# Attention beside a token-mixing MLP on one core: scores and product sums share four PSUM banks in turn, and the MLP's products are dealt evenly over the pairs of steps

## The chip, the core and the metric

One NeuronCore of a Trainium2 chip runs the whole program. The metric is the device time of one execution in microseconds; lower is better. Engines are named as the profile names them: PE (TensorE, matrix products; PEld are its weight loads), DVE (VectorE), ACT (ScalarE), POOL (GpSimd), SP (SyncE, which issues most DMAs). PE writes its results to PSUM, which has eight banks, each of 128 partitions by 512 float32 values; DVE or ACT reads a result from there, and only then may PE write to that bank again.

## What is computed

```python
x = A_x                                   # 2048 tokens x 512 channels
xn = _layernorm(x, axis=-1)
qkv = xn @ wqkv                           # 32 heads of 16
p = _softmax(q @ k.T * 16 ** -0.5)        # for each head, 2048 x 2048
s = (p @ v) @ wo
h = _layernorm(xn, axis=-1)
u = _gelu(h.T @ w1 + b1)                  # MLP across tokens, 2048 -> 1792
y = u @ w2 + b2                           # 1792 -> 2048
g = _silu(y.T)
out = x + s * g
```

Everything is float32. The big products are made three times, with an upper and a lower part of each factor (hi*hi, hi*lo, lo*hi), so one product of two blocks is three matmuls.

## The kernel before

**Stages.** First come the layer norms and the projections to q, k and v. Then a loop over steps in pairs, `for s in range(0, total + 1, 2)`. At step s the *maxima* of step s are made, and the *scores* of step t = s - 22, and the *values* of t - 2. From s = 22 to s = 510 every pair of steps has all of them; these are the 245 pairs that the change is about. Before them (s < 22) there are only maxima, behind them (s >= 512) only scores and values.

**One pair of steps** on PE is made of:

- eight maxima (`max_of`, L494): 48 x 128 by 48 x 512, into a bank of the pool `ps_mx`, which DVE reduces to a row maximum (L498). `ps_mx` has three banks.
- eight scores (`score`, L872): 50 x 128 by 50 x 512, into a bank of `ps_sc`, which ACT turns into exponentials (L877). `ps_sc` has three banks.
- two groups of values (`values`, L888), each of four matmuls in four column tiles (each of them two records in the trace), into the one bank of `ps_av`.
- zero to six products of the MLP or of the last projection (L1039), which are added up in the one bank of `ps_dn`. Each is made in two halves of 64 rows.

Maxima, scores and halves of products use 64 rows of the array or fewer. They are issued in *slots* of two, one for each half of the array's rows, and the two run at the same time. Which kinds stand in a pair's slots is written out by hand, as two strings for the two halves (D a product's half, m a maximum, s a score) and the two slots ahead of which a group of values stands. These rows are in `ORDERS`, and for pairs in which a sum ends or behind such a pair in `ENDS` and `BEGINS`. A pair with n products has 8 + n slots.

**Products.** `mixer()` yields the products of 14 sums of the first layer (48 products each) and of 16 sums of the second (42 each); `rest()` yields 13 sums of the last projection (9 each) and what comes after the loop. Ahead of the 245 pairs 177 products are done, and 1284 remain. A sum's end yields a function that reads the bank: `gelu` (first layer, ACT at L579, then POOL), `silu` (second layer) or `part` (last projection). Behind it `mixer` yields `None`, which ends the pair's share: the next sum starts in the next pair, since there is one bank for sums. `count` says how many products a pair takes: six, or four in pairs behind a sum's end and where seven or eight are left (in the fifth to the eighth sum always six).

**The second layer's input.** The results of the first layer go to DRAM (`store`, `u_d`) and come back to the tiles that held the first layer's input. The last of them comes back inside the first sum of the second layer, ahead of its last block: `mixer` waits there until it is stored, issues the load (L555), and yields `None` twice.

**Other work of DVE.** Every eighth pair ends a block of maxima. `max_rows` then reduces them (L513) and turns them by four 32 x 32 transposes (L510), in three pieces at the next three places ahead of values.

## Time and profile before

| | |
|---|---|
| median of 3 runs | 1676.91 us (1676.75 to 1678.35) |
| span of the profiled execution, first to last instruction | 1673.9 us |
| time of that execution outside the span | not in the record; the median is 3.0 us above the span |
| PE busy | 1658.1 us (99%) |
| DVE busy | 1428.2 us (85%) |
| ACT busy | 1200.1 us (72%) |
| POOL busy | 560.1 us (33%) |
| the 245 pairs | 206.35 to 1591.60 us, 1385.25 us |

Busy time of PE is the union of its instructions' spans. Matmuls are pipelined, and the spans that are shown overlap, so 99% busy does not mean that PE works at its peak: a matmul that starts late while an earlier one is still shown leaves no idle time in this number. The starts of the matmuls say more. In the views of windows, each row has the window, its length, and for each engine the busy time and the number of instructions.

### The profile page before, as it was taken

What the parts mean: (1) busy time and instruction counts of PE and PEld (TensorE: products, weight loads), DVE (VectorE), ACT (ScalarE), POOL (GpSimd) and SP (SyncE); (2) the same over time, 40 slices, a digit from 0 to 9 for tenths busy, and PEclk for the clock granted to TensorE, in tenths of its full rate; (3) what the DMA queues carried; (4) which work ended last, traced back from release to release, by engine and by line L of the source; (5) the groups of instructions that cost most, each with busy time, mean ns of one, the idle gap of its engine ahead of it and who ended that gap; (6) DMA issues with size and microseconds to landing.
All of it is one profiled execution on the core that took longest, in us unless ns stands there. A gap on an engine that the chain in (4) does not pass through costs nothing.

```text
span 1673.9 us, 30821 instructions
## 1 busy us (share of the span) xinstructions
PE 1658.1 (99%) x11754; PEld 874.6 (52%) x11754; DVE 1428.2 (85%) x2497; ACT 1200.1 (72%) x2300; POOL 560.1 (33%) x663
## 2 busy tenths in 40 slices
PE   9999999999999999999999999999999999999997
PEld 8887645454454445544444544445454444444443
DVE  7665988888888989889998989899898998899945
ACT  3333277777777777777877777777777778888875
POOL 0223853342234332342322322222223222642421
PEclk9999999999999999999999999999999999999999
DMA  6478621505142241916141513123142515363345
GB/s 231 178 239 188 130 65 46 92 28 85 39 72 60 50 68 34 242 55 105 36 83 39 95 49 53 48 54 66 36 67 62 84 37 93 117 124 103 115 143 201
DMA packets 152176, 155.30 MB, mean 93 GB/s; under 512 B 51596, under 2 KB 109964, under 8 KB 148956
## 3 DMA queue, kind: packets, MB, share of 16 engines
q1 hardware_dynamic: 147612, 152.59, 37.7%
q8 instruction: 92, 1.51, 0.4%
q0 software_dynamic: 4416, 0.75, 0.3%
q14 instruction: 56, 0.46, 0.1%
HBM read 101.86 MB, written 50.32 MB: 91 GB/s over the span
## 4 chain that ended last, share of the span: by engine, by line
PE 97%; DVE 2%; ACT 1%; issue 0%; DMA 0%; DVEq 0%; SPq 0%
PE av L888 30%; PE dn L1039 23%; PE mx L494 17%; PE sc L872 13%; PE dn L998 3%; PE mx L397 2%; PE sc L397 2%; DVE mxp L498 1%; PE av L998 1%; PE av L397 1%; PE dn L397 1%; PE mx L872 1%; PE sc L86 0%; PE sc L88 0%; PE sc L87 0%; PE mx L88 0%
## 5 line engine op out<-in xcount | busy, mean ns | idle before, releaser
L498 DVE TENSOR_REDUCE mxp<-mx 128x1 f32<-128x512 f32 x2004 | 1243.5, 682 | 146.7 <-PE mx L494 106.3
L877 ACT ACTIVATE prob<-sc 128x512 f32<-128x512 f32 x2004 | 1050.3, 604 | 300.5 <-PE sc L872 195.7
L872 PE MATMUL sc<-big 50*128 50x512 f32 x2004 | 755.5, 418 | 0.6
L494 PE MATMUL mx<-big 48*128 48x512 f32 x2004 | 744.5, 421 | 0.7
L888 PE MATMUL av<-prob,vp 128*32 128x512 f32 x4096 | 545.7, 605 | 0.0
L1039 PE MATMUL dn<-hu,wh 64*128 64x512 f32 x1556 | 538.9, 406 | 0.0
L494 PEld LDWEIGHTS mx<-big 48*128 48x128 f32 x2004 | 358.6, 185 | 284.0 <-DVE mxp L498 262.5
L872 PEld LDWEIGHTS sc<-big 50*128 50x128 f32 x2004 | 358.5, 185 | 102.0 <-ACT prob L877 82.5
L1039 PE MATMUL dn<-hu,wl 64*128 64x512 f32 x778 | 316.7, 407 | 0.0
L1039 PEld LDWEIGHTS dn<-hu,wh 64*128 64x128 f32 x1556 | 284.4, 184 | 44.4 <-issue 23.8
L1039 PEld LDWEIGHTS dn<-hu,wl 64*128 64x128 f32 x778 | 143.5, 185 | 108.0 <-issue 79.7
L888 PEld LDWEIGHTS av<-prob,vp 128*32 128x32 f32 x4096 | 80.8, 108 | 177.2 <-issue 166.1
L79 POOL TENSOR_TENSOR wl<-raw,wh 128x512 fp32r<-128x512 f32 x124 | 150.8, 1219 | 38.7 <-ACT wh L150 30.2
L148 POOL CAST wh<-raw 128x512 fp32r<-128x512 f32 (+1 forms) x107 | 62.1, 580 | 269.8 <-PE dn L1039 185.2
L521 POOL CAST m<-f 16x128 fp32r<-16x128 f32 x32 | 9.0, 280 | 278.6 <-DVE f L510 278.6
L580 POOL TENSOR_TENSOR sq<-u 128x512 f32<-128x512 f32 x14 | 14.6, 1041 | 178.4 <-ACT u L579 178.4
L83 POOL DMA_DIRECT2D big<-m x128 | 67.7, 535 | 0.0
L1039 PE MATMUL dn<-wh,hu 64*128 64x512 f32 x156 | 55.4, 408 | 0.0
L616 POOL TENSOR_SCALAR t<-t 128x512 f32<-128x512 f32 x16 | 23.8, 1490 | 79.8 <-ACT t L613 79.8
L79 POOL TENSOR_TENSOR hu<-hx,hu 128x512 fp32r<-128x512 f32 x16 | 20.4, 1292 | 67.1 <-ACT hu L255 67.1
L877 ACT ACTIVATE prob<-mx 128x512 f32<-128x512 f32 x44 | 27.4, 623 | 13.4 <-PE sc L872 11.5
L397 PE MATMUL mx<-xt,big 128*128 128x512 f32 x144 | 34.6, 389 | 0.0
(228 smaller groups left out, 1122.5 us busy)
## 6 DMA issues: line engine op xcount, KB each, us to landing
raw<-in_B_w_dram SPq DMA_DIRECT2D x104, 256.0 KB
big<-k_d SPq DMA_DIRECT2D x96, 128.0 KB
big<-q_d SPq DMA_DIRECT2D x96, 128.0 KB
q_d<-sg SPq DMA_DIRECT2D x16, 512.0 KB
k_d<-sg SPq DMA_DIRECT2D x16, 512.0 KB
num_d<-ev SPq DMA_DIRECT2D x30, 256.0 KB
u_d<-uo SPq DMA_DIRECT2D x14, 512.0 KB
hu<-u_d SPq DMA_DIRECT2D x14, 512.0 KB
```

Of the source, the lines that this page charges most:

```text
L79: eng.tensor_tensor(out=o, in0=a, in1=b.bitcast(F32), op=OP.subtract)
L83: queue.dma_start(dst.bitcast(F32), src.bitcast(F32))
L148: nc.gpsimd.tensor_copy(whs[n][:, :m, :], raws[n][:, :m, :])
L397: nc.tensor.matmul(ps, w[part][:, kd, m], xt[kd][:, z, :], start=w is wh and z == 0 and kd == 0, stop=w is wl and kd == ND - 1,)
L494: nc.tensor.matmul(ps, q[o : o + 48, r * P : (r + 1) * P], k[o : o + 48, c * 512 : (c + 1) * 512], start=True, stop=True,)
L498: nc.vector.tensor_reduce(mxp[u // 16][:, a, r % 8, c : c + 1], ps, axis=AX.X, op=OP.max)
L616: nc.gpsimd.tensor_scalar(t, t, 1.0, None, op0=OP.add)
L872: nc.tensor.matmul(ps, ks[p][o : o + 50, kb * P : (kb + 1) * P], qs[p][o : o + 50, at : at + 512], start=True, stop=True,)
L877: nc.scalar.activation(e, ps, AF.Exp, scale=scale)
L888: nc.tensor.matmul(av[32 * j : 32 * j + 32, :], vps[p][:, kb, 16 * a : 16 * a + 32], prob.pop((t, a, c)), start=kb == 0, stop=kb == NB - 1,)
L998: nc.tensor.matmul(ps, w(slice(0, P)), m(slice(0, P)), start=first, stop=last)
L1039: made.append(lambda r=r, start=first and a == lead, stop=last and a != lead: nc.tensor.matmul(ps, w(r), m(r), start=start, stop=stop,))
```

## The change

1. **Four banks in turn.** `ps_sc` (three banks) and `ps_dn` (one) become a ring of four pools of one bank each. `turn()` hands out the next bank of the ring and leaves out banks on which a sum is under way. A sum takes its bank (`Sum`) when its first product is issued, and keeps it until its last one is issued (`let_go`).
2. **No break at a sum's end.** The `None` behind a sum is gone in the 245 pairs, so that the next sum can start in the same or the next pair.
3. **Even shares.** `plan` works out ahead of the pairs by which pair each sum is to end, evenly, and the 13 sums of the last projection by two pairs each; `count` takes what is left of the sum by the pairs that are left to it, at most six.
4. **New orders.** `MIDST`, `BEGIN` (behind a pair in which a sum ended) and `END` (such a pair) take the place of `ORDERS`, `BEGINS` and `ENDS`.
5. **The last load of the second layer's input** is issued at the first block of products at which it is stored, and no `None` follows it.

The number of pairs with n products, before: 149 with six, 14 with five, 79 with four, and one each with three, one and none. After: 72 with six, 160 with five, 13 with four. The sum is 1284 both times.

```diff
-    ps_sc = pool("ps_sc", 3, space=PSUM)
+    ring = [pool(f"ps_{i}", 1, space=PSUM) for i in range(4)]
     ps_mx = pool("ps_mx", 3, space=PSUM)
     ps_av = pool("ps_av", 1, space=PSUM)
-    ps_dn = pool("ps_dn", 1, space=PSUM)
...
+    def turn(lasting=False):
+        while True:
+            place[0] = (place[0] + 1) % 4
+            if place[0] not in summing:
+                break
+        if lasting:
+            summing.append(place[0])
+        return ring[place[0]].tile([P, 512], F32, name="sc")
+
+    class Sum:
+        def __init__(self, of=lambda: turn(True)):
+            self.of, self.ps = of, None
+        def __call__(self):
+            if self.ps is None:
+                self.ps = self.of()[:, :D]
+            return self.ps
...
-                if i == NF and kb == NF - 1:
-                    while NF - 1 not in stored:
+                if i == NF and len(ub) < NF:
+                    while kb == NF - 1 and NF - 1 not in stored:
                         yield None
-                    ub.append(hu.tile([P, 2, D], F32R, name="hu"))
-                    move(ub[NF - 1], u_d[NF - 1])
-                    yield None
-                    yield None
+                    if NF - 1 in stored:
+                        ub.append(hu.tile([P, 2, D], F32R, name="hu"))
+                        move(ub[NF - 1], u_d[NF - 1])
...
-            yield (lambda i=i, ps=ps: gelu(i, ps)) if i < NF else (lambda i=i, ps=ps: silu(i - NF, ps))
-            if i + 1 >= min(N_BEFORE, NF):
-                yield None
+            yield let_go((lambda i=i, ps=ps: gelu(i, ps())) if i < NF else (lambda i=i, ps=ps: silu(i - NF, ps())), not (before and i % 2))
+
+    def let_go(f, lasting=True):
+        def then():
+            if lasting:
+                summing.pop(0)
+            f()
+        return then
...
-        6: ("DDDDDDsmmsmsms", "msmssmmsDDDDDD", 4, 8),
+        5: ("DDDDDmmssmsms", "msmsmssmDDDDD", 5, 8),
...
+    END = {5: ("DDDDDssmmsmsm", "smsmsmmsDDDDD", 5, 8), 6: ("DDDDDDsmssmmsm", "smsmmsmsDDDDDD", 7, 14)}
...
+    def plan():
+        left = -done
+        of = []
+        for n in sizes:
+            left += n
+            if left > 0:
+                of.append(left)
+                left = 0
+        pairs = (NU - LEAD) // 2 - 2 * PARTS
+        n = pairs / sum(of[:-PARTS])
+        at = 0
+        for i, size in enumerate(of):
+            at += size
+            short = i - len(of) + PARTS + 1
+            last_pairs.append((done + at, pairs + 2 * short if short > 0 else round(at * n)))
...
-        if i in FULL:
-            return max(0, min(6, left))
-        return 4 if late or left in (7, 8) else 5 if left == 9 else max(0, min(6, left))
+        end, pair = last_pairs[0]
+        return min(6, (end - done) // max(1, pair - k))
```

The order on PE shows it at two places and the one on SP at a third. Names are as the program gives them: `mx` a bank for a maximum, `sc` one for a score (and, after the change, for a sum too), `dn` a sum's bank before, `av` the values' bank, `big` the tiles of q and k, `hu` the MLP's input, `wh` and `wl` the upper and lower part of its weights.

**First place: PE, a common pair in the second layer's sums, from behind the first group of values to the first matmul of the second.** Before (a pair with six products):

```order
L1039 MATMUL dn_14345<-hu_9176,wl_14349 128x512
L872 MATMUL sc_14704<-big_1495,big_1496 128x512
L1039 MATMUL dn_14345<-hu_9255,wh_14348 128x512
L494 MATMUL mx_14709<-big_1386,big_1385 128x512
L872 MATMUL sc_14712<-big_1495,big_1496 128x512
L494 MATMUL mx_14716<-big_1386,big_1385 128x512
L494 MATMUL mx_14719<-big_1386,big_1385 128x512
L872 MATMUL sc_14722<-big_1495,big_1496 128x512
L888 MATMUL av_14214<-prob_14624,vp_12874 32x512
```

After, in the same pair, which now has five:

```order
L524 MATMUL mx_14693<-big_1392,big_1391 128x512
L908 MATMUL sc_14696<-big_1501,big_1502 128x512
L524 MATMUL mx_14700<-big_1392,big_1391 128x512
L908 MATMUL sc_14703<-big_1501,big_1502 128x512
L908 MATMUL sc_14707<-big_1501,big_1502 128x512
L524 MATMUL mx_14711<-big_1392,big_1391 128x512
L924 MATMUL av_14200<-prob_14655,vp_12862 32x512
```

Between the two groups of values four slots became three: no product stands there any more, and three maxima follow each other in successive slots.

**Second place: PE, the end of the fifth sum of the first layer and the start of the next.** Before:

```order
L494 MATMUL mx_3058<-big_1496,big_1495 128x512
L1039 MATMUL dn_2412<-hu_153,wh_2497 128x512
L494 MATMUL mx_3062<-big_1496,big_1495 128x512
L1039 MATMUL dn_2412<-hu_153,wh_2497 128x512
L494 MATMUL mx_3066<-big_1496,big_1495 128x512
L1039 MATMUL dn_2412<-hu_153,wl_2498 128x512
L888 MATMUL av_2939<-prob_2947,vp_1667 32x512
L888 MATMUL av_2939<-prob_2965,vp_1667 32x512
L888 MATMUL av_2939<-prob_2986,vp_1667 32x512
L888 MATMUL av_2939<-prob_2995,vp_1667 32x512
L1039 MATMUL dn_3080<-hu_138,wh_2669 128x512
L494 MATMUL mx_3088<-big_1496,big_1495 128x512
```

After:

```order
L524 MATMUL mx_3133<-big_1502,big_1501 128x512
L1076 MATMUL sc_2424<-hu_159,wh_2578 128x512
L908 MATMUL sc_3137<-big_1391,big_1392 128x512
L1076 MATMUL sc_2424<-hu_159,wh_2578 128x512
L524 MATMUL mx_3142<-big_1502,big_1501 128x512
L1076 MATMUL sc_2424<-hu_159,wl_2579 128x512
L924 MATMUL av_2942<-prob_3056,vp_1673 32x512
L924 MATMUL av_2942<-prob_3065,vp_1673 32x512
L924 MATMUL av_2942<-prob_3017,vp_1673 32x512
L924 MATMUL av_2942<-prob_3028,vp_1673 32x512
L1076 MATMUL sc_3156<-hu_144,wh_2751 128x512
L524 MATMUL mx_3158<-big_1502,big_1501 128x512
```

The tiles of the two sums, sc_2424 and sc_3156, are both on the ring's fourth bank, as dn_2412 and dn_3080 were on one bank before: the score ahead of them had the third, so it is the fourth's turn. A score (sc_3137) now stands two slots ahead of the sum's last product, where there were maxima alone.

**Third place: SP, the last store of the first layer's results (`u_d13`) and its load.** Before:

```order
L83 DMA u_d13_105<-uo_9777 128x1024
L139 DMA raw_9912<-in_B_w2_dram 128x4x128
L139 DMA raw_10083<-in_B_w2_dram 128x2x128
L83 DMA hu_10161<-u_d13_105 128x1024
L638 DMA d_8870<-ev_10229 16x1x64 x2
```

After:

```order
L168 DMA raw_10025<-in_B_w2_dram 128x4x128
L112 DMA u_d13_111<-uo_10057 128x1024
L112 DMA hu_10109<-u_d13_111 128x1024
L674 DMA d_8813<-ev_10162 16x1x64 x2
L678 DMA num_d1_1_117<-ev_10162 128x512
```

The load now stands right behind the store, with no load of weights between them, and the stores of an attention block follow it in the queue.

More of the change, by code (lines that the diff above doesn't have):

```diff
@@ L997, in whole @@
         ps, w, m, first, last = x
[L998 to L1004 removed]
+        nc.tensor.matmul(ps(), w(slice(0, P)), m(slice(0, P)), start=first, stop=last)
+    MIDST = {
         0: ("ssmmmssm", "msmssmms", 3, 8),
@@ L1021, in order @@
-    def order(n, t, late, ends):
-        of = BEGINS[done > n_fill or t % NB == 2] if late else ENDS if ends else ORDERS
-        n = min(x for x in ORDERS if x >= n)
-        return of.get(n, ORDERS[n])
-    def halves(lead, n):
-        parts, then = ([], []), []
-        def each(x, f):
-            if f:
-                then.append(f)
-                return
-            ps, w, m, first, last = x
-            for a, made in ((lead, parts[0]), (1 - lead, parts[1])):
-                r = slice(64 * a, 64 * a + 64)
-                made.append(lambda r=r, start=first and a == lead, stop=last and a != lead: nc.tensor.matmul(
-                    ps, w(r), m(r), start=start, stop=stop,
-                ))
-        take(n, each)
-        return *parts, then
+        4: ("smDDDDsmsmsm", "msmsmsmsDDDD", 1, 7),
@@ L1060, in items, with count @@
+    def count(s):
+        k = (s - LEAD) // 2
+        if not last_pairs:
+            plan()
+        while last_pairs and last_pairs[0][0] <= done:
+            last_pairs.pop(0)
+        if not last_pairs:
+            return 0
+        end, pair = last_pairs[0]
+        return min(6, (end - done) // max(1, pair - k))
     def items(s, a):
@@ L1096, in tile_attention_token_mixer @@
             steady[0] = True
-            late = ended[0]
-            one, two, then = halves(lead, count(late))
+            one, two = halves(lead, count(s))
             made = [dict(D=part, m=heads[a][0], s=heads[a][1]) for part, a in ((one, lead), (two, 1 - lead))]
-            first, second, *places = order(len(one), t, late, bool(then))
+            of = BEGIN if begun else END if ended[0] else MIDST
+            begun = ended[0]
+            n = len(one)
+            n = min(x for x in MIDST if x >= n)
+            first, second, *places = of.get(n, MIDST[n])
             if one:
@@ L1113, in tile_attention_token_mixer @@
                         of[kind].pop(0)()
-                if "D" in kinds and not two:
-                    for f in then:
-                        f()
-                    then = []
-            for f in then:
-                f()
         elif s < NU:
```

104 lines of the change are left out of this document (67 added, 37 removed).

## The prediction

> **What bounds the kernel now.** I read the page first: the span, and the chain of work that ended last by engine.
>
> ```profile
> span 1673.9 us, 30821 instructions
> ...
> PE 97%; DVE 2%; ACT 1%; issue 0%; DMA 0%; DVEq 0%; SPq 0%
> ```
>
> The chain is PE almost alone. That doesn't say that PE is never late, since its spans overlap. So I took the starts of the pairs' first matmuls from the timeline and cut the 245 pairs, and one cycle of eight of them, into windows (length, then busy time and count of each engine, granted clock, DMA).
>
> ```profile
> 206.35:1591.60 1385.25, 1383.96 (x10393) 679.83 (x10394) 1244.38 (x2118) 1081.48 (x2070) 472.00 (x560) 1.00 0.34 73
> ...
> 1057.41:1063.41 6.00, 6.00 (x47) 2.88 (x46) 5.49 (x11) 4.35 (x9) 3.17 (x7) 1.00 0.01 2
> 1063.41:1069.09 5.68, 5.68 (x47) 2.90 (x44) 4.96 (x9) 4.14 (x9) 2.37 (x4) 1.00 0.00 1
> 1069.09:1074.75 5.66, 5.66 (x47) 2.93 (x45) 4.95 (x9) 4.71 (x10) 1.08 (x1) 1.00 0.01 3
> 1074.75:1079.98 5.23, 5.23 (x43) 2.61 (x42) 4.72 (x9) 4.12 (x9) 0.45 (x1) 1.00 0.40 127
> 1079.98:1085.52 5.54, 5.52 (x42) 2.54 (x41) 4.86 (x9) 4.70 (x10) 1.45 (x2) 1.00 0.00 1
> 1085.52:1090.82 5.30, 5.30 (x43) 2.50 (x39) 5.07 (x9) 4.64 (x10) 3.84 (x4) 1.00 0.20 66
> 1090.82:1096.71 5.89, 5.89 (x46) 2.96 (x45) 5.17 (x9) 4.26 (x9) 0.00 (x0) 1.00 0.27 77
> 1096.71:1102.41 5.70, 5.70 (x47) 2.88 (x43) 5.33 (x13) 4.14 (x9) 0.00 (x0) 1.00 0.00 0
> sum 45.00, PE 44.98 PEld 22.21 DVE 40.55 ACT 35.06 POOL 12.36; mean PE 5.62 PEld 2.78 DVE 5.07 ACT 4.38 POOL 1.55
> ```
>
> A pair with six products has 44 matmul records and with four 40; the counts run a few over, as neighbours' spans reach in. Calm pairs show what PE needs: **5.67 with six products** (rows two and three) and **5.23 with four** (row four), so 0.22 for one product. Other pairs with the same work take 6.00, 5.89, 5.54. The eight hold 5 x 6 + 3 x 4 = 42 products and would take 5 x 5.67 + 3 x 5.23 = 44.04 if all were calm; 0.96 is lost. For whom PE waits stands in the groups (line, engine, operation, tiles, count | busy, mean ns | idle before, releaser):
>
> ```profile
> L494 PEld LDWEIGHTS mx<-big 48*128 48x128 f32 x2004 | 358.6, 185 | 284.0 <-DVE mxp L498 262.5 <-issue 0.7 <-DVE neg L513 0.4
> L872 PEld LDWEIGHTS sc<-big 50*128 50x128 f32 x2004 | 358.5, 185 | 102.0 <-ACT prob L877 82.5 <-ACT u L579 0.8
> ...
> L1039 PE MATMUL dn<-hu,wh 64*128 64x512 f32 x1556 | 538.9, 406 | 0.0
> ...
> L1039 PE MATMUL dn<-hu,wl 64*128 64x512 f32 x778 | 316.7, 407 | 0.0
> ...
> L1039 PE MATMUL dn<-wh,hu 64*128 64x512 f32 x156 | 55.4, 408 | 0.0
> ...
> L1039 PE MATMUL dn<-wl,hu 64*128 64x512 f32 x78 | 30.4, 389 | 0.0
> ```
>
> Weight loads of maxima sat 262.5 us until DVE had cleared a bank, those of scores 82.5 until ACT had. Much of it is hidden behind matmuls, but the split tells where the loss is: banks of maxima first, banks of scores second.
>
> **The floor.** The four lower rows count 1556 + 778 + 156 + 78 = 2568 halves, 1284 products, in both kernels. All pairs calm: 245 x 5.23 + (1284 - 980) x 0.22 = 1281.4 + 66.9 = **1348.2**. The new deal gives the same by pairs, 160 x 5.45 + 72 x 5.67 + 13 x 5.23. The stage took 1385.25, so **37.0 us are waits**, and this is all that parts 1 to 4 of the change can win. Ahead of the stage and behind it PE's instructions stand in the same order by kind, and no engine has more or fewer of a kind in all; I count nothing there.
>
> **What the change leaves of the 37.** I add up what will still wait.
>
> (a) *Maxima in the common pair* (160 with five). The calm pair shows the rhythm:
>
> ```profile
> 1065.45 0.49 PE L872 MATMUL sc<-big 50*128 50x512 f32 x1
> ...
> 1065.79 0.40 PE L494 MATMUL mx<-big 48*128 48x512 f32 x1
> ...
> 1066.24 4.96 DVE L498 TENSOR_REDUCE mxp<-mx 128x1 f32<-128x512 f32 x8 [0.72 <-PE mx L494]
> ...
> 1066.59 1.06 PE L888 MATMUL av<-prob,vp 128*32 128x512 f32 x8
> ...
> 1067.58 0.50 PE L494 MATMUL mx<-big 48*128 48x512 f32 x1
> ...
> 1067.92 0.39 PE L872 MATMUL sc<-big 50*128 50x512 f32 x1
> ```
>
> From the values' start to the slot behind them it takes 1.0, from that slot to the next 0.34, from the slot ahead of values to the one behind them some 1.35 ((c) has it: 268.01 to 269.34); other slots are 0.23 apart, which makes the calm pair of five 5.45 again. The reduce starts 0.45 behind its maximum; eight reduces take 4.96, so (4.96 - 0.68) / 7 = 0.61 each, the last one 0.68. In the new order the maxima stand in slots 0, 2, 4, then 5, 6, 7 behind the first values, then 9 and 11: at 0, 0.46, 0.92, 2.28, 2.62, 2.85, 4.52, 4.99, and the next pair begins at 5.45. DVE's reduces then start at 2.83, 3.44, 4.05 (the three), 4.97, 5.58, and for the next pair 6.19, 6.80, 7.41, and then DVE waits for 8.28. A maximum needs the bank of the third one before it. The tightest is the third of the next pair, at 6.37: its bank is read from 5.58 to 6.26. **0.11 to spare**, all others have more. So the common pair is calm, by my walk, and DVE idles 0.5 of 5.45.
>
> (b) *DVE's other work*, once in eight pairs:
>
> ```profile
> L513 DVE TENSOR_REDUCE neg<-mxp 128x16 f32<-128x64 f32 x32 | 7.0, 218 | 0.8
> ...
> L510 DVE STREAM_TRANSPOSE f<-neg 32x32 f32<-32x32 f32 x128 | 25.6, 200 | 6.0 <-DVE neg L513 0.5
> ```
>
> One reduce (0.22) and four transposes (0.20 each) come in three pieces, 0.45, 0.4 and 0.2 with their gaps, 1.05 together. Before, the pair with the last piece took 6.00, 0.33 over calm. Bounds: nothing, as the idle 0.5 of a pair takes each piece up; or all of 1.05, 32 us over 30.6 cycles. I take 0.2 a cycle, **6.1 us**, nearer to nothing: the first piece is 0.45 and the idle time at its place about half of that. With five products a pair is 0.22 shorter than before and DVE has that much less room, so this part does not vanish.
>
> (c) *Sum's end.* Before, ACT frees the bank in the shadow of values:
>
> ```profile
> 268.01 0.39 PE L1039 MATMUL dn<-hu,wl 64*128 64x512 f32 x1
> ...
> 268.34 1.07 PE L888 MATMUL av<-prob,vp 128*32 128x512 f32 x8
> 268.48 0.69 ACT L579 ACTIVATE u<-dn,b1t 128x512 f32<-128x512 f32 x1
> ...
> 269.34 0.50 PE L1039 MATMUL dn<-hu,wh 64*128 64x512 f32 x1
> ...
> 1062.68 2.56 ACT L877 ACTIVATE prob<-sc 128x512 f32<-128x512 f32 x5 [0.76 <-PE dn L1039]
> ```
>
> ACT read it 0.47 behind the last product and was done at 269.17, and the next sum's product came at 269.34. After, in the first eleven sums of the stage the ring's turn falls on the bank just left: scores take the three others in turn, and the place behind the last score's is the old sum's. And four scores stand in the seven slots ahead of the sum's end, whose exponentials ACT takes first, 0.49 apart (last row: five in 2.56, the last 0.6). Counted from the first of these scores: last product at 1.48, exponentials from 0.55 to 2.5, the read from 2.5 to 3.2, the next product due at 1.48 + 1.36 = 2.84. Late by 0.4, ten times; and once (the pair with five, no values between) by 1.2. **5.2 us**; bounds 0 and 11 x 1.2 = 13. In later sums the turn falls on another bank and I count nothing: the old one is next wanted by a score, 2.1 behind the last product, when ACT has read it at 1.7 (in the last projection's pairs 1.6, behind a shorter queue of exponentials).
>
> Here the Trainium skill, Perfetto Trace Analysis, section Matmuls under Optimizing Tensor Performance, says that independent matmul groups should rotate through different banks, so that one's evacuation overlaps the next one's matmuls. The ring is meant so, yet the order shows that eleven sums don't rotate; by the rule as it stands this term would be nothing and the time 1651.
>
> (d) *ACT's extra work* (casts of the divided blocks, L702, tanh) delays exponentials in places:
>
> ```profile
> 1446.59:1452.94 6.35, 6.24 (x43) 2.56 (x42) 5.22 (x9) 6.30 (x13) 5.24 (x5) 1.00 0.15 43
> ...
> 753.02:769.28 16.26, 16.00 (x106) 6.64 (x105) 14.62 (x24) 13.14 (x26) 1.44 (x2) 1.00 0.49 75
> ```
>
> ```profile
> 1446.40 0.63 ACT L613 ACTIVATE t<-ev 128x512 f32<-128x512 f32 x1
> ...
> 1446.94 0.60 ACT L702 CAST hu<-u 128x512 fp32r<-128x512 f32 x1
> ```
>
> This pair with four products took 6.35, 1.1 over calm, behind a tanh and a cast. The casts are as many as before, and the ring gives scores no more banks than they had: four, less the sum's. Bounds 0 and eight such pairs, 9 us; I take half, **4.5**.
>
> (e) *The last load.* The second row above holds the three pairs with one, no and three products: 16.26 where four products and calm would be 3 x 5.23 - 8 x 0.22 = 13.9. This 2.3 is part of the 37 and goes, if the load is in time:
>
> ```profile
> 712.21 0.71 ACT L579 ACTIVATE u<-dn,b1t 128x512 f32<-128x512 f32 x1
> ...
> 727.38 0.34 SPq L83 DMA_DIRECT2D u_d<-uo  x1
> ...
> 732.02 0.67 SPq L83 DMA_DIRECT2D hu<-u_d  x1
> ```
>
> ACT read the first layer's last sum at 712.21; the store was issued at 727.38, 15 us on, and the load 4.6 later, when the store had landed. The new sum lasts 8 pairs, 44 us, and wants that block in its last, 38 us on. So some 15 us of cover are left; without it the 2.3 stay. Weights are loaded and split two quarters (24 products, five pairs) ahead as before. SP waits those 4.6 us right behind the store; queued there are the attention block's stores and the load of q and k for a head pair that is 16 pairs off.
>
> **Sum.** 1348.2 + 6.1 + 5.2 + 4.5 = 1364.0, so 21.2 less than 1385.25. The span goes from 1673.9 to 1652.7. The median of the runs lies 3.0 above the profiled span; I keep that and say **1656**. What can't be told from no change is some 0.2%, 3.4 us.
>
> **Rivals.**
>
> *Nearly calm* (chance 0.18): pieces and casts fall into DVE's and ACT's idle time and only (c) stays: 1348.2 + 5.2 + 2, 1647. For it: the idle 0.5 a pair. Against: before, with 0.7 idle in a six-pair (5.67 less 4.96), pieces still cost.
>
> *The ring doesn't rotate, and scores are no better off* (0.19): all of (c)'s and (d)'s upper bounds, 13 + 9 with 6.1, 1376, so 1668. For it: eleven same banks in the order, no more banks for scores. Against: the four-products pairs whose waits on ACT were largest are nearly gone.
>
> *The waits come back in part* (0.07): a loss of 35 us again, by many small ones, ends within 0.2%.
>
> *DVE takes the bound, and it is slower* (0.05): the third maximum of the common pair has 0.11 to spare. If DVE runs 0.31 behind my walk, each of the 160 pairs waits 0.2, 32 us: 1688. It decides from a wait of 21.2 / 160 = 0.13 in each. For it: 262.5 us of waits of that kind now, and three maxima in successive slots. Against: DVE idles in each pair, so that it can't fall behind for long.
>
> *The clock* (0.01):
>
> ```profile
> 1591.60:1673.90 82.30, 69.69 (x405) 31.65 (x401) 40.20 (x71) 49.84 (x100) 15.80 (x20) 0.96 0.53 173
> ```
>
> Where PE idles (69.7 of 82.3 busy) the granted clock is 0.96; at that clock the stage would take 1364 / 0.96 = 1421, and the kernel 1713. The Trainium skill, TensorE: Matmul & The Clock Gate, section "A second HAM failure mode: psum-queue depth-cycling", tells of a kernel that cycled through PSUM banks, idled a little between groups, and lost its clock. The trace goes against it: three banks cycle in it already, and the stage is granted 1.00.
>
> **Chances.** My forecast (1651 to 1661) 0.50, nearly calm 0.18, a smaller gain 0.19: faster 0.87. Same 0.07. Slower 0.06. Range: 1645 to 1672, from nearly calm to past the rival at 1668; it leaves out the calm floor itself, no change and slower.
>
> **What would show it.** In the windows, common pairs of 5.45 with 42 records; if they read 5.55 or more, (a) is wrong, and the idle of maxima's weight loads behind DVE says by how much. A pair's start behind a sum's end in the first eleven sums late by 0.4, with ACT's read of the sum just ahead of it (c). Pairs with the pieces near 5.65 (b). No pair with fewer than four products and no wait for the load (e). The stage's length, 1364, is the sum's test; a change ahead of it or behind it would mean that my "nothing" there is wrong.

## The result and the profile after

The changed kernel takes **1659.7 us** (median of four runs, 1659.3 to 1660.1), the kernel before beside it 1677.0 (1676.8 to 1678.4). The ratio is 0.9896, interval 0.9882 to 0.991. The forecast was 1656 in a range of 1645 to 1672: the direction and the range held, and the time is 3.7 us above the forecast.

From the page, the span, and of the costliest groups the three that tell for whom PE waits (line, engine, operation, tiles, count | busy, mean ns | idle before, releaser):

```profile
span 1657.6 us, 30903 instructions
...
L1076 PE MATMUL sc<-hu,wh 64*128 64x512 f32 x1556 | 505.7, 399 | 5.0 <-ACT u L615 4.6
L524 PEld LDWEIGHTS mx<-big 48*128 48x128 f32 x2004 | 351.7, 185 | 283.2 <-DVE mxp L528 265.2
L908 PEld LDWEIGHTS sc<-big 50*128 50x128 f32 x2004 | 352.1, 185 | 168.2 <-ACT prob L913 149.0
```

The weight loads of maxima still sat 265.2 us until DVE had read a bank, and those of scores 149.0 until ACT had, more than before (82.5). Yet the kernel is faster, since this idle time of the loader lies beside running matmuls. One thing is new: PE itself stood 4.6 us until ACT had read a sum (L615). That is small, but it is no idle time of the loader: nothing covers it.

The stage of the 245 pairs, what lies behind it, and a cycle of eight pairs with 42 products, as in the eight shown of before (window, length, busy time and count on PE, PEld, DVE, ACT, POOL; clock; DMA):

```profile
206.77:1574.77 1368.00, 1362.56 (x10393) 700.96 (x10392) 1245.25 (x2118) 1069.13 (x2070) 474.97 (x567) 1.00 0.34 74
1574.77:1657.60 82.83, 71.56 (x405) 32.97 (x403) 39.88 (x71) 50.30 (x102) 11.77 (x14) 0.95 0.54 175
...
1084.91:1090.34 5.43, 5.43 (x45) 2.90 (x43) 5.25 (x13) 4.14 (x9) 0.00 (x0) 1.00 0.33 97
1090.34:1096.08 5.74, 5.74 (x45) 2.80 (x43) 5.46 (x10) 4.23 (x9) 2.47 (x6) 1.00 0.02 4
1096.08:1101.50 5.42, 5.42 (x44) 2.88 (x42) 4.96 (x9) 4.13 (x9) 2.17 (x3) 1.00 0.01 2
...
1106.92:1112.36 5.44, 5.44 (x46) 2.88 (x42) 4.98 (x9) 4.24 (x9) 1.70 (x2) 1.00 0.80 151
1112.36:1118.05 5.69, 5.69 (x47) 2.96 (x45) 4.97 (x9) 4.15 (x9) 0.00 (x0) 1.00 1.01 118
1118.05:1123.79 5.74, 5.74 (x46) 2.83 (x42) 5.50 (x10) 5.08 (x11) 1.90 (x2) 1.00 1.11 118
1123.79:1129.33 5.54, 5.54 (x47) 2.75 (x44) 4.52 (x8) 4.35 (x9) 3.86 (x4) 1.00 0.54 136
sum 44.42, PE 44.42 PEld 22.84 DVE 40.62 ACT 34.74 POOL 12.30; mean PE 5.55 PEld 2.86 DVE 5.08 ACT 4.34 POOL 1.54
```

The stage, cut at the first matmul behind it as before, fell from 1385.25 to 1368.00, by 17.25. What lies behind it took 0.5 longer (82.83, was 82.30), and what lies ahead 0.4 (206.77, was 206.35). The cycle took 44.42 where 45.00 stood. Its common pairs take 5.42 to 5.44. One pair with five products takes 5.74: it is the one behind DVE's first pieces of the row maxima, and DVE's busy 5.46 is the highest of the pairs with five.

All the pairs, by kind, from the starts of their first matmuls (the last pair of the stage is left out; it took 5.52). "Over" is the sum of what they took above 5.23, 5.45 and 5.67. The three columns on the right are kernels of the experiments below.

| pairs | count | after: mean | over | skips the bank (e1) | that and even pieces (e9) | short reduces (e10) |
|---|---|---|---|---|---|---|
| five products, common | 122 | 5.475 | 3.0 | 3.3 | -1.6 | -3.9 |
| five, behind a sum's end | 24 | 5.537 | 2.1 | 2.1 | 2.1 | 2.0 |
| five, a sum ends | 13 | 5.612 | 2.1 | 0.8 | 0.8 | 2.0 |
| six, common or behind an end | 46 | 5.70 | 1.5 | 1.5 | 1.1 | 0.3 |
| six, a sum ends | 26 | 5.925 | 6.6 | 2.1 | 1.9 | 4.5 |
| four | 13 | 5.567 | 4.4 | 4.6 | 4.0 | 1.1 |
| all | 244 | | 19.7 | 14.4 | 8.3 | 6.0 |

The kernel before was 37.0 over by the same reckoning: its 79 pairs with four lost 14.2, its 149 with six 16.9, its 14 with five 3.5, and the three odd ones 2.3. So the gain lies in the pairs with four, of which 13 are left, and in those with six, of which 72 are left; the many new pairs with five cost little. Of the pairs with six in which a sum ends, the first ten take 6.22 in the mean and the others 5.72 to 5.76.

The floor is somewhat too high. The first of the 245 pairs has no values yet, other than the list of stages says, and takes 4.28 (4.27 before); and a calm pair of five takes 5.43 rather than 5.45. That is why the row of common pairs with five can fall below zero: the first pair alone makes it 1.2 lower (1.7 in e10).

### The profile page after: what moved, and what is told of

Read it like the earlier page. It is cut to its first block, busy times and chain, and to the rows that moved or that the text cites. A ratio compares the mean times of both kernels' runs of the same rounds, so it can differ in the third digit from the quotient of the medians.

```text
span 1657.6 us, 30903 instructions
## 1 busy us (share of the span) xinstructions
PE 1638.6 (99%) x11754; PEld 896.0 (54%) x11754; DVE 1429.0 (86%) x2497; ACT 1188.2 (72%) x2300; POOL 558.9 (34%) x663
## 4 chain that ended last, share of the span: by engine, by line
PE 94%; ACT 3%; DVE 2%; DMA 1%; POOL 1%; issue 0%; SPq 0%; DVEq 0%; ACTq 0%; POOLq 0%
PE av L924 29%; PE sc L1076 21%; PE mx L524 17%; PE sc L908 13%; PE sc L1033 3%; PE sc L427 3%; PE mx L427 2%; ACT prob L913 2%; DVE mxp L528 1%; PE av L1033 1%; PE av L427 1%; PE mx L908 1%; PE sc L115 0%; PE sc L117 0%; PE sc L116 0%; ACT u L615 0%
## 5 line engine op out<-in xcount | busy, mean ns | idle before, releaser
L524 PE MATMUL mx<-big 48*128 48x512 f32 x2004 | 752.4, 418 | 0.2
L908 PE MATMUL sc<-big 50*128 50x512 f32 x2004 | 736.9, 418 | 0.2 <-ACT prob L913 0.2
L1076 PE MATMUL sc<-hu,wh 64*128 64x512 f32 x1556 | 505.7, 399 | 5.0 <-ACT u L615 4.6
L524 PEld LDWEIGHTS mx<-big 48*128 48x128 f32 x2004 | 351.7, 185 | 283.2 <-DVE mxp L528 265.2
L908 PEld LDWEIGHTS sc<-big 50*128 50x128 f32 x2004 | 352.1, 185 | 168.2 <-ACT prob L913 149.0
L1076 PE MATMUL sc<-hu,wl 64*128 64x512 f32 x778 | 313.2, 403 | 0.0
L1076 PEld LDWEIGHTS sc<-hu,wh 64*128 64x128 f32 x1556 | 281.3, 185 | 52.3 <-issue 24.8
L1076 PEld LDWEIGHTS sc<-hu,wl 64*128 64x128 f32 x778 | 143.3, 184 | 13.0
L1076 PE MATMUL sc<-wh,hu 64*128 64x512 f32 x156 | 52.5, 390 | 0.0
L427 PE MATMUL sc<-xt,big 128*128 128x512 f32 x192 | 46.1, 389 | 0.0
L427 PEld LDWEIGHTS sc<-xt,big 128*128 128x128 f32 x192 | 36.0, 188 | 7.5
```

Of the source, the lines that this page charges most:

```text
L427: nc.tensor.matmul(ps, w[part][:, kd, m], xt[kd][:, z, :], start=w is wh and z == 0 and kd == 0, stop=w is wl and kd == ND - 1,)
L524: nc.tensor.matmul(ps, q[o : o + 48, r * P : (r + 1) * P], k[o : o + 48, c * 512 : (c + 1) * 512], start=True, stop=True,)
L908: nc.tensor.matmul(ps, ks[p][o : o + 50, kb * P : (kb + 1) * P], qs[p][o : o + 50, at : at + 512], start=True, stop=True,)
L1076: nc.tensor.matmul(ps(), w(r), m(r), start=first and a == lead, stop=last and a != lead)
```

## The experiments

### Sums that skip the bank just left (e1)

```diff
-            if place[0] not in summing:
+            if place[0] not in summing and not (lasting and place[0] == left_bank[0]):
...
-                summing.pop(0)
+                left_bank[0] = summing.pop(0)
```

> The changed kernel (1659.7 us), with one difference: a new sum does not take the bank that the sum before it has just left. Theory A (in eleven sums the first product waits for ACT to read the bank that it takes again): the ten pairs that end a sum of the first layer go from 6.20 to the 5.75 of the later sums, and the one early pair of 6.69 to about 5.5, so 10 x 0.45 + 1.2 = 5.7 us less, about 1654.0. Rival (these pairs are long for another reason, the order of their maxima or the values at their end): within 1 us of 1659.7.

The theory was right: it took **1654.42** (1654.32 to 1654.84; ratio 0.9867, 0.9852 to 0.9882), 5.3 less. The fifth sum's end in the timeline of the changed kernel (start, length, engine, what; in brackets the idle time before):

```profile
272.42 0.39 PE L1076 MATMUL sc<-hu,wl 64*128 64x512 f32 x1
...
272.74 1.06 PE L924 MATMUL av<-prob,vp 128*32 128x512 f32 x8
273.35 0.71 ACT L615 ACTIVATE u<-sc,b1t 128x512 f32<-128x512 f32 x1
...
274.21 0.47 PE L1076 MATMUL sc<-hu,wh 64*128 64x512 f32 x1 [0.40 <-ACT u L615]
```

The sum's last product begins at 272.42, ACT's read, behind the exponentials, at 273.35, and the next sum's first product at 274.21: 1.47 from the start of values to the next slot, where 1.0 is usual. The same place with the skip:

```profile
272.01 1.06 PE L925 MATMUL av<-prob,vp 128*32 128x512 f32 x8
272.62 0.71 ACT L616 ACTIVATE u<-sc,b1t 128x512 f32<-128x512 f32 x1
...
273.00 0.49 PE L1077 MATMUL sc<-hu,wh 64*128 64x512 f32 x1
```

Here the product comes 0.99 behind the start of values, while ACT is still reading the old sum. All 26 ends with six products fall to 5.72 to 5.81, and the group row of PE's idle time behind L615 is gone. So the first eleven sums did go back to the bank just left, and that cost what the prediction's term said.

### Sums on one fixed bank (e2)

```diff
-                ps = Sum()
+                ps = Sum(lambda: ring[3].tile([P, 512], F32, name="sc"))
```

The same edit stands at the last projection's sums, and the fourth bank is kept out of the turn from the start.

> The changed kernel, with the sums on one fixed bank and the scores on the three others, as before the change; dealing, orders and early load stay. Theory A (the gain is in the even dealing and the orders; the ring only saves the wait at a sum's end): 15 more sums of the two layers pay the 0.45 us that the first ten pay already, 6.8 us, and the sums of the last projection nothing, since values lie between: about 1666.5, still some 10 us faster than before the change. Rival (the ring is what gains): most of the 17.3 us lost, 1672 or more.

**1667.64** (ratio 0.9945, 0.993 to 0.996), 7.9 slower than the changed kernel, near the number expected. Now each end waits, those of the second layer too:

```profile
L1077 PE MATMUL sc<-hu,wh 64*128 64x512 f32 x1556 | 505.3, 399 | 11.0 <-ACT ev L648 6.0 <-ACT u L615 4.6 <-issue 0.4
```

PE's 11.0 us of idle time are put down to the reads of both layers' sums, 4.6 (L615) and 6.0 (L648), where the changed kernel had the 4.6 alone. The rotation is worth 13.2 us (1667.64 less 1654.42), of which the changed kernel had 7.9.

### Four and six in turn (e3)

```diff
-        return min(6, (end - done) // max(1, pair - k))
+        n = min(6, (end - done) // max(1, pair - k))
+        return n if n != 5 or end - done < 9 else 4 if k % 2 else 6
```

> The changed kernel, with pairs of four and six products in turn in place of two pairs of five (76 pairs of four among them in place of 13), the ring and the orders kept. Theory A (even shares matter: eight maxima take DVE 4.96 us, a pair of four is calm at 5.23 and leaves it almost no room, and the pairs of four in the changed kernel take 5.41 even where nothing else disturbs): 63 more pairs of four at 0.17 to 0.3 us over calm, some at pieces of max_rows more, 11 to 19 us: 1671 to 1679. Rival (only the sums' ends and the orders matter): within 3 us of 1659.7.

**1686.99** (ratio 1.0061, 1.0045 to 1.0078): the direction was right, but the loss of 27.3 against the changed kernel is more than the 11 to 19 expected. (The run has 86 pairs of four, where the expectation counted 76; at 0.17 to 0.3 for each of 73 more that would be 12 to 22, still too little.) Three pairs in windows (six, four and six products), and the maxima's weight loads among the groups:

```profile
938.68:944.71 6.03, 6.03 (x46) 2.87 (x45) 5.33 (x9) 4.98 (x10) 0.44 (x1) 1.00 0.01 3
944.71:950.01 5.30, 5.30 (x42) 2.52 (x40) 4.60 (x9) 4.08 (x9) 1.46 (x2) 1.00 0.72 141
950.01:956.05 6.04, 6.04 (x47) 2.87 (x45) 5.34 (x9) 4.41 (x9) 0.00 (x0) 1.00 1.04 117
```

```profile
L524 PEld LDWEIGHTS mx<-big 48*128 48x128 f32 x2004 | 352.6, 185 | 440.9 <-DVE mxp L528 418.9 <-issue 1.4 <-DVE neg L543 0.4
```

The pairs with four products take 5.30, near their calm 5.23, but those with six behind them take 6.03 instead of 5.67. The loads wait 418.9 us for DVE, 154 more than in the changed kernel. So the mean of a four and a six is not a five: what DVE doesn't finish in the shorter pair, PE waits for in the longer one.

### The old order in the common pair (e6)

```diff
-        5: ("DDDDDmmssmsms", "msmsmssmDDDDD", 5, 8),
+        5: ("DDDDDmmsmsmss", "mmsmsssmDDDDD", 5, 8),
```

> The changed kernel, with the order that pairs of five products had before the change in 122 of the 160 pairs of five. Theory A (with five products DVE has room in either order; by the walk the tightest maximum has 0.1 us to spare in both): within 3 us of 1659.7. Rival (the new orders carry the gain): 122 pairs of 0.1 us more or over, 1672 or more.

**1672.87** (1672.09 to 1675.19; ratio 0.9977, 0.9968 to 0.9986): the theory that the shares alone matter missed, and the rival's size came out, though not in the way it was put. An old pair of five behind another old one takes 5.44 as a rule, as the new one does. The loss is where the old order meets one that was not taken back. Pair by pair against the changed kernel, the 24 old pairs of five right behind a pair in the `BEGIN` order lose 5.7 us in all (5.67 instead of 5.44), and the 24 pairs with six right behind an old pair lose 4.4. These are 10.1 of the 12.8 us that the pairs lose. The end of a common pair and the start of one with six behind it, in the timeline:

```profile
941.75 0.39 PE L908 MATMUL sc<-big 50*128 50x512 f32 x1
...
942.18 2.06 ACT L913 ACTIVATE prob<-sc 128x512 f32<-128x512 f32 x4 [0.50 <-PE sc L1076]
942.22 0.39 PE L908 MATMUL sc<-big 50*128 50x512 f32 x1
...
942.45 0.39 PE L908 MATMUL sc<-big 50*128 50x512 f32 x1
...
942.83 0.18 PEld L908 LDWEIGHTS sc<-big 50*128 50x128 f32 x1 [0.19 <-ACT prob L913]
```

The old order ends with scores in two successive slots and the next pair, from 942.68, begins with one: three in a row. Beside the sum's bank the ring has three for scores, so the score at 942.83 needs the bank of the one at 941.75. ACT takes that one up only at 942.18, and four exponentials take it 2.06, so the weight load of the last score waits 0.19 for ACT. The pair takes 5.90, as do most with six behind an old pair (5.65 to 5.70 in the changed kernel, where no piece of DVE disturbs). At the other seam maxima crowd. At the start of the pair from 1004.87, behind one in the `BEGIN` order, maxima begin at 1004.42, 1004.89 and 1005.12. They have the three banks, and the load of the next one waits for DVE:

```profile
1005.72 0.18 PEld L524 LDWEIGHTS mx<-big 48*128 48x128 f32 x1 [0.19 <-DVE mxp L528]
```

So the 13.2 us are mostly the price of an order that does not fit its neighbours: a new one that begins and ends with maxima and scores by turns meets neither wait. What the old order costs among old ones only is not shown.

### DVE's pieces twice as long (e4)

```diff
-                nc.vector.transpose(f[:, 32 * c : 32 * c + 32], neg[32 * c : 32 * c + 32, :])
+                for _ in range(2):
+                    nc.vector.transpose(f[:, 32 * c : 32 * c + 32], neg[32 * c : 32 * c + 32, :])
```

> The changed kernel, with each of the 128 transposes of max_rows made twice (0.20 us each, 0.8 us more of DVE in eight pairs, 25 us in all). Theory A (DVE's 0.5 us of idle time a pair takes up part of such work; the eight pairs lost some 0.35 us to 1.05 us of it): each cycle loses more than before but less than what is added, 0.3 to 0.6 us, 9 to 18 us: 1669 to 1678. Rival 1 (it is all on the path): 25 us, 1685. Rival 2 (the waits in these pairs are from something else than DVE's pieces): within 3 us of 1659.7.

**1679.61** (1679.38 to 1681.42; ratio 1.0019, 1.001 to 1.0028): 19.9 slower than the changed kernel for 25.6 us of transposes added (128 of 0.2), just outside the theory's range and below the rival's number. So some 0.8 of each us added goes through to the end, and a piece costs nothing only within a small room. One pair in each cycle carries most of it, such as this one:

```profile
967.60:973.91 6.31, 6.02 (x44) 2.78 (x42) 6.08 (x14) 4.23 (x9) 2.22 (x5) 1.00 0.01 3
```

It took 6.31, with DVE busy 6.08 of it; the same pair took 5.61 in the changed kernel. Common pairs stayed at 5.40 to 5.46.

### The last load late (e5)

```diff
-                if i == NF and len(ub) < NF:
-                    while kb == NF - 1 and NF - 1 not in stored:
+                if i == NF and kb == NF - 1:
+                    while NF - 1 not in stored:
                         yield None
-                    if NF - 1 in stored:
-                        ub.append(hu.tile([P, 2, D], F32R, name="hu"))
-                        move(ub[NF - 1], u_d[NF - 1])
+                    ub.append(hu.tile([P, 2, D], F32R, name="hu"))
+                    move(ub[NF - 1], u_d[NF - 1])
+                    yield None
+                    yield None
```

> The changed kernel, with the second layer's last load as late as before the change and with its breaks, so that three pairs take three, no and three products. Theory A (the late load costs the waits of pairs with few products, 2.3 us before): 1661 to 1663. Rival (the early load is worth nothing, since products are only moved): within 1 us of 1659.7.

**1663.36** (ratio 0.992, 0.9906 to 0.9933), 3.7 slower, just above what was expected. The pair with no products and the second one behind it are the dear ones:

```profile
772.96:779.37 6.41, 6.06 (x36) 2.12 (x33) 6.27 (x13) 4.76 (x10) 0.69 (x1) 1.00 0.60 187
784.45:791.00 6.55, 6.45 (x47) 2.96 (x46) 5.57 (x10) 5.17 (x11) 4.21 (x5) 1.00 0.01 1
```

The first took 6.41 where 5.23 - 4 x 0.22 = 4.35 would be calm, with DVE busy 6.27: without products the eight reduces and the pieces are longer than PE's own work. The other, with six products, took 6.55, 0.9 over.

### DVE's pieces dealt anew (e7, e8, e9)

All three are made from the kernel that skips the bank. Its pieces are the reduce with one transpose, two transposes, one transpose; the POOL work and the DMAs of the row maxima (`m`, `big`) follow the last. In e7 they are spread over five places, in e8 over four, in e9 again over three, but with the first one lighter:

```diff
-            turned(0)
...
-            turned(3)
+            turned(2, 3)
...
-        return first_, lambda: turned(1, 2), last
+        return first_, lambda: turned(0, 1), last
```

> The rotating sums of e1, and DVE's work of max_rows in five pieces of 0.2 us (the reduce, then one transpose at each of four places, the last with the rest) in place of three of 0.45, 0.4 and 0.2. Theory A (a piece that fits into DVE's idle time at its place, some 0.25 us, costs nothing): the pairs with pieces go from 5.74 to near 5.5, 0.2 a cycle, 6 us less than e1: about 1648. Rival (the last piece comes two places later, and the scores that need its rows then wait for POOL and its DMA, 4.5 us for 5.5 of cover): 1654 or more.

**1702.48** (1700.58 to 1707.68; ratio 1.0155, 1.0141 to 1.0169): the rival was right. Each place more puts the DMAs off by half a pair, and the scores come due before they have landed:

```profile
L908 PE MATMUL sc<-big 50*128 50x512 f32 x2004 | 743.0, 422 | 36.1 <-DMA big<-m 35.2 <-ACT t L844 0.6 <-ACT prob L913 0.2
```

PE stood 35.2 us for `big<-m` ahead of scores; in the changed kernel that group's idle time was 0.2 us.

> The same with four pieces: the reduce, one transpose, two transposes, the last. Theory A: between e1 and e7, 3 us less than e1, about 1651, as one piece of 0.4 us stays. Rival (the place of the pieces in the pair matters, not their size): as e1, 1654.

**1655.53** (1654.90 to 1661.12; ratio 0.9881, 0.9867 to 0.9895), no gain over e1. Most pairs with the pieces did become calm (5.42 to 5.45), but in the profiled run two pairs waited for the late DMAs, 7.23 and 10.07. The second one, in windows, in the timeline, and the DMA view of these 21 us (queue, count, KB each, median us from issue to landing):

```profile
690.24:695.66 5.42, 5.42 (x45) 2.88 (x42) 4.96 (x9) 4.12 (x9) 4.42 (x7) 1.00 0.80 220
695.66:705.73 10.07, 7.42 (x45) 3.16 (x43) 5.08 (x9) 4.64 (x10) 0.20 (x1) 0.83 0.31 120
705.73:711.19 5.46, 5.46 (x45) 2.85 (x42) 4.98 (x9) 4.24 (x9) 1.70 (x2) 1.00 0.84 289
```

```profile
690.66 2.13 POOL L113 DMA_DIRECT2D big<-m  x4
...
698.93 0.46 PE L908 MATMUL sc<-big 50*128 50x512 f32 x1 [2.65 <-DMA big<-m]
...
700.03 1.32 PE L924 MATMUL av<-prob,vp 128*32 128x512 f32 x8
...
702.86 1.67 PE L924 MATMUL av<-prob,vp 128*32 128x512 f32 x8
```

```profile
hu<-u_d SPq DMA_DIRECT2D x6, 512.0 KB
...
big<-m POOLq DMA_DIRECT2D x4, 4.0 KB, 6.3
```

POOL issued the four small DMAs from 690.66 on, while the DMA engines were 0.80 busy with 512 KB loads. They took 6.3 us to land, where the median of all 128 is 1.6, and PE stood 2.65 us for them. The two pairs cost 1.8 and 4.6 us. Without them the profiled run (1655.34) would, as an estimate, have taken 1649, so that the rival's number came out for another reason than the rival's, and the run does not decide between the two.

> The kernel with the ring that skips the bank just left (1654.4), and DVE's pieces of the row maxima dealt anew over the same three places: the reduce alone (0.22), two transposes (0.40), two transposes (0.40) and what follows, so that the DMAs of the row maxima are issued where they were. A (a piece costs what it exceeds DVE's idle time of some 0.25 to 0.4 at its place): the pairs with the first piece fall from 5.74 to about 5.55 and the time to 1650 (1648.5 to 1652.5). Rival (what a piece costs is set by its being there, not by its length, or the last piece with 0.40 now costs what the first one saves): 1654 to 1655.

**1648.58** (1648.01 to 1650.16; ratio 0.9835, 0.9821 to 0.9848): the theory was right, and this is the fastest version that leaves nothing out, 11.1 below the changed kernel and 28.2 below the kernel before beside it (1676.81). What the first piece does, from DVE's timeline and the maxima's weight loads in the cycle shown above of the changed kernel:

```profile
1087.53 0.22 DVE L543 TENSOR_REDUCE neg<-mxp 128x16 f32<-128x64 f32 x1
1087.86 0.20 DVE L540 STREAM_TRANSPOSE f<-neg 32x32 f32<-32x32 f32 x1
1087.99 1.83 DVE L528 TENSOR_REDUCE mxp<-mx 128x1 f32<-128x512 f32 x3
1089.85 0.41 DVE L540 STREAM_TRANSPOSE f<-neg 32x32 f32<-32x32 f32 x2
1090.20 3.03 DVE L528 TENSOR_REDUCE mxp<-mx 128x1 f32<-128x512 f32 x5
```

```profile
1091.49 0.18 PEld L524 LDWEIGHTS mx<-big 48*128 48x128 f32 x1 [0.26 <-DVE mxp L528]
```

From 1087.53 to 1093.23 DVE hardly rests. The reduce and three transposes stand in it, the last reduces of the run end 8.3 behind the pair's start (1084.91), and at 1091.49 the load of a maximum waits 0.26 for DVE. That wait is not covered: the pair begins at 1090.34 and its first values at 1091.92, 1.58 on, where the common pair ahead of it needs 1.27, and 0.31 is all that the pair loses. The same place in e9, whose pair starts at 1076.33:

```profile
1078.96 0.22 DVE L544 TENSOR_REDUCE neg<-mxp 128x16 f32<-128x64 f32 x1
1079.13 1.89 DVE L529 TENSOR_REDUCE mxp<-mx 128x1 f32<-128x512 f32 x3
1080.94 0.40 DVE L541 STREAM_TRANSPOSE f<-neg 32x32 f32<-32x32 f32 x2
1081.28 3.06 DVE L529 TENSOR_REDUCE mxp<-mx 128x1 f32<-128x512 f32 x5
1084.37 0.41 DVE L541 STREAM_TRANSPOSE f<-neg 32x32 f32<-32x32 f32 x2
```

One transpose less stands ahead, the same run of reduces ends 8.0 behind the start, and the pair behind takes 5.43. The transpose has gone to the third place, which holds 0.41 now, and costs nothing there.

### Short reduces (e10, e11)

```diff
-        nc.vector.tensor_reduce(mxp[u // 16][:, a, r % 8, c : c + 1], ps, axis=AX.X, op=OP.max)
+        nc.vector.tensor_reduce(mxp[u // 16][:, a, r % 8, c : c + 1], ps[:, :256], axis=AX.X, op=OP.max)
...
-        nc.scalar.activation(e, ps, AF.Exp, scale=scale)
+        nc.scalar.activation(e, ps, AF.Exp, scale=scale * 0.125)
```

> The changed kernel, but each row maximum is taken over the first 256 of its 512 columns, so that DVE's reduces are shorter; the exponent is scaled down by eight to keep it finite, at no change of instructions. The other half of the columns is left out of the maxima. A (of the 19.7 us over the floor, DVE's room holds the pieces and part of the seams, some 10 to 12): pairs with pieces are calm, maxima's weight loads hardly wait for DVE, and the time is 1647 to 1651; what is left is the sum's end and ACT. Rival (the order on PE itself sets the seams, whatever DVE does): 1654 or more.

> The kernel with pairs of four and six products in turn, with the same shorter reduces (half of the columns left out of the maxima, exponent scaled down by eight). With whole reduces it was 27.3 us slower than the changed kernel. A (the loss is DVE's: a six-pair behind a four-pair finds DVE late): it comes within 4 us of the changed kernel with shorter reduces. Rival (the order of slots at the seam between a four-pair and a six-pair costs it, on PE alone): it stays 20 to 30 us behind that one.

**1645.93** for e10 (ratio 0.9817, 0.9803 to 0.983), one us below the theory's range, and **1648.42** for e11 (ratio 0.9831, 0.9817 to 0.9844). With shorter reduces, four and six in turn are 2.5 us behind the even shares instead of 27.3: the loss in e3 was DVE's, not that of slots on PE. A pair with pieces in e10, and the reduces among its groups:

```profile
818.51:823.95 5.44, 5.44 (x44) 2.68 (x42) 3.42 (x10) 4.14 (x9) 3.18 (x8) 1.00 0.20 56
```

```profile
L528 DVE TENSOR_REDUCE mxp<-mx 128x1 f32<-128x256 f32 x2004 | 797.4, 422 | 571.1 <-PE sc L908 224.8 <-PE sc L1076 154.6 <-PE mx L524 126.8
```

A reduce takes 422 ns where it took 681, DVE is busy 3.42 of 5.44, and the pair is calm. One sign that was expected did not come: the weight loads of maxima still sat 203.2 us until DVE had read a bank (265.2 in the changed kernel; 323.7 in e11). E10's column in the table is not zero: the ends of sums on the bank just left stay (4.5 and 2.0), and so do the pairs behind an end.

## Why the forecast was right, and by how much it missed

Step by step, over the calm floor:

**The floor** held: in e9 common pairs with five take 5.41 to 5.46 (5.45 worked out), with six 5.65 to 5.70, and the whole stage is within 8.3 us of it.

**(a) Common pair calm:** right. The common pair takes 5.43, and with short reduces no less, so it loses nothing to DVE. The 0.11 to spare was not too little. The rival "DVE takes the bound" named a real mechanism at a point where this kernel isn't: e3 brings it about. That e3 lands at 1687 where the rival said 1688 is luck, since the loss there is 0.36 in each pair with six behind one with four, not 0.2 in each pair with five.

What I read from the idle time of the weight loads was wrong as a measure. It was to tell where the loss lies and by how much. But the loads of maxima sat 262.5 us before and 265.2 after, while 17 us were gained, and 203.2 in e10, where the pairs with pieces are calm. That maxima come first is shown by e10, which takes 13.7 of the 19.7 us away by short reduces alone.

**(b) DVE's pieces:** 6.1 forecast. Laying them out anew saved 6.1 by the table (14.4 less 8.3) and 5.8 by the medians, and six pairs of 5.60 to 5.63 are left in e9, 1 us more. The size was about right, though it isn't 0.2 in every cycle: of the thirty cycles twelve lose 0.25 to 0.3 in one pair, six lose 0.15 to 0.2 in each of two pairs, and the others less.

**(c) Sum's end:** 5.2 forecast, 5.3 measured by e1. The ten late ends and the single one of 6.69 are where the order put them. The Trainium skill's rule (Perfetto Trace Analysis, Matmuls) agrees with e1 and e2: groups that rotate through banks don't wait (the 4.6 us that PE stood behind L615 are gone in e1, and e2 has 10.6 behind L615 and L648). What the kernel's own ring lacked was to skip the bank just left, and this was read from the order, not from the number of pools.

**(d) ACT's extra work:** this step failed, though its number looks right. I took 4.5 for exponentials held up by casts and tanh. The 13 pairs with four products are indeed dear, 4.4 over calm. But with short reduces they lose 1.1 with the same casts, and eleven of the thirteen take 5.23 to 5.25. There it is DVE's room, eight reduces in the shortest of pairs, and not ACT. Only the two that still take 5.74 and 5.70 in e10, which hold 1.0 of that 1.1, show the mechanism that I had named. In the first of them (from 1420.96) ACT made a tanh and two casts between exponentials, 0.60 to 0.63 each, and a score stood for its bank:

```profile
1424.01 0.49 PE L908 MATMUL sc<-big 50*128 50x512 f32 x1 [0.18 <-ACT prob L913]
```

So the term of 4.5 was some 1 us of ACT, and that the sum of these pairs came near it is luck.

What made the forecast too low are the seams at a sum's end, which apart from (c) I counted at nothing: in e9 they hold 2.1 in the pairs behind an end and 2.7 in those with one. What the changed kernel lost beyond (b) and (c) is 19.7 + 0.1 (the last pair) - 6.1 - 5.3 = 8.4, against the 4.5 of (d). The difference, 3.9, is nearly all of what the stage (1368.0) lies above the forecast (1364.0). The pairs behind an end take 5.53 with short reduces as well, so DVE isn't their cause, and the trace shows no wait there either. Such a pair differs from a common one in its first slot, which stands right behind the values that end the pair before: in e10 it lasts 0.34 (984.68 to 985.02), where 0.23 is usual (1001.07 to 1001.30), and the slots behind it are alike. The later ends with six fall from 5.74 to 5.67 with short reduces, so theirs is DVE's. Why the ends with five take 5.51 stays open.

**(e) The last load:** right, it was in time and the pairs with one, no and three products are gone. Put back, they cost 3.7; the 2.3 counted only the three pairs, and a pair behind them lost 0.9 too.

**The rest:** "nothing" ahead of the stage and behind it was short by 0.4 and 0.5. The span came out 4.9 above the forecast (1657.6, not 1652.7). The median lies 2.1 above the profiled span, not 3.0, so that 0.9 of the miss does not show in it, which is luck.

The clock stayed at 1.00 through the stage, so the rival of the clock is out. Of the other rivals, "the ring doesn't rotate" was true of eleven sums, and "nearly calm" needs what e9 does.

Taken back one at a time, the order of the common pair costs 13.2 (e6), the turn of banks 7.9 (e2), the load 3.7 (e5), and the even shares, in the form of e3, 27.3. These are more than the 17.3 gained, so the parts are not independent, and e6 also makes seams between old and new orders that neither kernel has. Part 2 of the change, no break at a sum's end, was not taken back by itself, and which pairs of parts are worth what was not tried.

## What to carry to other kernels

Where one engine is full and a second nearly so, look at the seams and not at the mean: the second engine's short extra work is free only as long as it fits into the idle time at its place, and 0.2 us moved by half a pair made 5.8 us. Share work evenly between equal periods if the second engine's load per period is fixed. And a ring of buffers rotates only if the place it hands out next isn't the one just given up: print the order and see which bank the next group gets. An order of slots is judged with its neighbours: scores or maxima that crowd across a seam cost 0.2 us a pair here, with an order that is calm among its own kind.

## What the runs showed of the hardware

In e8 a stop of PE was dearer than its length. In the window 695.66 to 705.73 PE stood 2.65 us, up to 698.93, and the granted clock of the window is 0.83, between two windows of 1.00. Cut finer, the clock is 1.00 up to 700.70 and then half for 3.4 us:

```profile
700.72:704.12 3.40, 3.40 (x18) 1.03 (x14) 2.12 (x4) 1.58 (x3) 0.00 (x0) 0.50 0.00 0
```

The two groups of values that reach into it took 1.32 and 1.67 us, 1.06 elsewhere. The pair lost 10.07 - 5.45 = 4.6: the stop itself, and most of the rest by the halved clock (3.4 us at half are worth 1.7). The other stop for these DMAs in that run, 1.35 us (430.30), left the clock at 1.00 in its window. In e7, where such stops are many, the mean clock of the profiled run was 0.99 (0.998 in the changed kernel).

Four DMAs of 4 KB took 6.3 us to land beside six loads of 512 KB, where the median of all 128 is 1.6; that the loads held them up was not tried. In the changed kernel, which issues the small ones half a pair earlier, they took 2.1 us to land in the same stretch (685 to 706, with six such loads too), and PE's idle time ahead of scores is 0.2 us in all.
